# Strassen's algorithm for the second product of an MLP, chunks 1 to 5, in a gated-attention kernel

## The chip, the cores and the metric

The kernel runs on one core of a Trainium2 chip. The metric is the device time of one execution in microseconds. Five engines work side by side, each with a queue of its own that it runs in order: TensorE (PE; its weight loads are listed apart as PEld), VectorE (DVE), ScalarE (ACT), GpSimd (POOL) and SyncE (SP), which here issues the DMAs. They wait for each other through semaphores, which a compiler sets from the program's reads and writes.

## What is computed

A gated linear attention over 768 steps (4 batches, 8 heads of 48), then a layer norm and an MLP with a residual, all in float32; the weights arrive as float64 words and are rounded on the chip.

```python
for t in range(S):
    state = alpha[:, :, t, :, None] * state + np.einsum('bhd,bhe->bhde', k[:, :, t], v[:, :, t])
    y[:, :, t] = np.einsum('bhd,bhde->bhe', q[:, :, t], state)
...
x = np.ascontiguousarray(attn_out.transpose(0, 2, 1, 3)).reshape(B, S, H * D)
xn = (x - mu) / np.sqrt(var + 1e-06) * g_ln
ch = np.maximum(xn @ w_ch1, 0.0) @ w_ch2
return (x + ch).astype(np.float32)
```

Here `x` is 4 x 768 x 384, `w_ch1` is 384 x 1536 and `w_ch2` is 1536 x 384. The change concerns the product by `w_ch2`.

## The kernel before

The 768 steps are cut into six chunks (NCB = 6) of 128 tokens, which is one tile of 128 partitions. For a chunk `c` and a batch `b`, attention goes through five steps:

- `decays` (L184): logarithms of the gates, a prefix sum as a matmul with a triangle of ones (L190), two exponentials on ACT, and the scaled q on DVE (L196) and k on POOL (L195). It also issues the loads of the next chunk.
- `turn` (L206): eight transposes on PE (L211) into two PSUM tiles, copied out into `qkT`.
- `scores` (L219): 48-row matmuls (L226) and two masked copies on DVE (L229).
- `attend` (L233): the output (L240, L245), the new state (L252, L255, L257), `x`, and its layer norm `xn` (L263 to L269).
- `turn_x` (L273): three transposes of `xn` into `xT`.

The MLP of a chunk has twelve `hidden` steps (L284): step `j` multiplies 128 columns of `w1` with the tokens of all four batches, three matmuls of 512 columns (L289), and writes the relu into row `j` of `hT` (ACT at L292, DVE at L294). `hT` is one tile of 128 partitions by [12 j, 4 batches, 128 tokens] with one buffer. `project` (L298) then computes, for one batch, the 128 x 384 output: twelve matmuls (L302), each with a 128 x 128 block of `hT` as the stationary operand and 384 columns of `w2[:, j]` as the moving one, summed in one PSUM tile. It is done in thirds of four matmuls, two batches taking turns. After the last third DVE adds `x` (L306), and SP sends the row out (L307). PSUM has three buffers with the tag `m` for the outputs of `hidden` and `project`, and three with the tag `a` for attention.

The order is written by hand. `run(main, side)` (L325) issues the list `main` and strews the list `side` evenly into it, at most one side step behind each main step here. For chunk `c`, `main` is the projection of `c` and then the hidden steps of `c + 1` (12 + 12 steps), and `side` is the attention of chunk `c + 2` (20 steps), as long as there is one: chunks 0 to 3 have side steps, 4 and 5 have none. Ahead of that loop (L344) stand the attention of chunk 0, the rounding of the weights (`round_weights`, L122, on DVE, six pieces of `w1` and six of `w2`) together with the hidden steps of chunk 0, and the attention of chunk 1 as side steps. The compiler keeps this order as a priority; an engine's instructions may be put ahead of others that would still wait.

Of the kernel before, what the change touches and what calls it, by code (L numbers as in the profile page):

```python
# [9 lines left out]
FP32 = mybir.dt.float32  # L10
INT32 = mybir.dt.int32
UINT32 = mybir.dt.uint32
INT64 = mybir.dt.int64
# [8 lines left out]
def kernel(  # L22
# [8 lines left out]
    w_ch2: bass.AP,  # L31
    out: bass.AP,
):

# [17 lines left out]
    nc = tc.nc  # L54

    B, S, H, D = q.shape
    DM = H * D
    DF = w_ch1.shape[1]
    P = 128
    NCB = S // P  # L60
    NP = H // 2
    R = 64 + D
    NF = DM // P
    NJ = DF // P
# [5 lines left out]
    stage = ctx.enter_context(tc.tile_pool(name="stage", bufs=STAGED))  # L70
    work = ctx.enter_context(tc.tile_pool(name="work", bufs=2))
    dram = ctx.enter_context(
        tc.tile_pool(name="dram", bufs=B, space=bass.MemoryType.DRAM))
    ps = ctx.enter_context(tc.tile_pool(name="ps", bufs=2, space=bass.MemoryType.PSUM))
# [24 lines left out]
    w2 = cpool.tile([P, NJ, DM], FP32, name="w2")  # L99
# [7 lines left out]
    for i in range(NJ // 2):  # L107
        cs, js = slice(2 * i * P, 2 * (i + 1) * P), slice(2 * i, 2 * (i + 1))
# [71 lines left out]
    gate_of, qkT_of, at_of, x_of, xn_of, xT_of, hT_of = ({} for _ in range(7))  # L180
# [23 lines left out]
            load(c + 1, b)  # L204

    def turn(c, b):  # L206
        qkT = work.tile([R, 2, NP, P], FP32, name="qkT", tag="qkT", bufs=3)
        for i in range(2):
            tps = ps.tile([R, NP, P], FP32, name="tps", tag="a", bufs=3)
            for p in range(NP):  # L210
                nc.tensor.transpose(  # L211
                    tps[:, p], qks[b][:, i, p].rearrange("p a b -> p (a b)")[:, :R], ident)
            if i == 0 or c == 1:
                nc.scalar.copy(out=qkT[:, i], in_=tps)  # L214
            else:
                nc.vector.tensor_copy(out=qkT[:, i], in_=tps)
        qkT_of[c, b] = qkT
# [15 lines left out]
    def attend(c, b):  # L233
        qkT, at, vt = qkT_of.pop((c, b)), at_of.pop((c, b)), raws.pop(("v", c, b))
        yps = ps.tile([P, NP, 2, D], FP32, name="yps", tag="s")
        sides = [slice(64 * s, 64 * s + 64) for s in range(2)]
        for p in range(NP):
            if c > 0:
                for s in sides:
                    nc.tensor.matmul(yps[s, p].rearrange("p a b -> p (a b)"), qkT[:, 0, p, s],  # L240
                                     sts[b][:R, p].rearrange("p a b -> p (a b)"),
                                     start=True, stop=False)
            for i in range(2):
                for s in sides:
                    nc.tensor.matmul(yps[s, p, i], at[:, i, p, s], vt[:, 2 * p + i],  # L245
                                     start=(c == 0), stop=(c == 0 or i == 1))
        if c + 1 < NCB:
            sps = ps.tile([R, NP, D], FP32, name="sps", tag="s")
            heads = list(enumerate((slice(0, 64), slice(64, R))))
            for p in range(NP):  # L250
                for i, s in heads:
                    nc.tensor.matmul(sps[s, p], qks[b][:, 1, p, i, :s.stop - s.start],  # L252
                                     vt[:, 2 * p + i], start=True, stop=True)
            for i, s in heads:
                nc.vector.tensor_add(sts[b][s, :, i], sps[s], sts[b][s, :, i])  # L255
            st = sts[b].rearrange("p a b d -> p a (b d)")
            nc.gpsimd.tensor_mul(  # L257
                st, st, gate_of.pop((c, b)).unsqueeze(2).broadcast_to([P, NP, 2 * D]))
        x = work.tile([P, DM], FP32, name="x", tag="x", bufs=3 * B)
        nc.scalar.copy(out=x, in_=yps.rearrange("p a b d -> p (a b d)"))  # L260
        stats = work.tile([P, 6], FP32, name="stats", tag="stats")
        mv = work.tile([P, 2], FP32, name="mv", tag="mv")
        nc.vector.bn_stats(stats, x)  # L263
        nc.vector.bn_aggr(mv, stats)
        rstd = work.tile([P, 1], FP32, name="rstd", tag="rstd")
        nc.scalar.activation(out=rstd, in_=mv[:, 1:2], func=AFT.Ln, bias=eps)
        nc.scalar.activation(out=rstd, in_=rstd, func=AFT.Exp, scale=-0.5)
        xn = work.tile([P, DM], FP32, name="xn", tag="xn", bufs=2)
        nc.vector.tensor_scalar(out=xn, in0=x, scalar1=mv[:, 0:1], scalar2=rstd,  # L269
                                op0=AOP.subtract, op1=AOP.mult)  # L270
        x_of[c, b], xn_of[c, b] = x, xn
# [12 lines left out]
    def hidden(c, j):  # L284
        if j == 0:
            hT_of[c] = work.tile([P, NJ, B, P], FP32, name="hT", tag="hT", bufs=1)
        hps = ps.tile([P, B, P], FP32, name="hps", tag="m", bufs=3)
        for f in range(NF):
            nc.tensor.matmul(hps, w1[:, f, j * P:(j + 1) * P], xT_of[c][:, f],  # L289
                             start=(f == 0), stop=(f == NF - 1))  # L290
        if c == 0 or j % 2 == 0:
            nc.scalar.activation(out=hT_of[c][:, j], in_=hps, func=AFT.Relu)  # L292
        else:
            nc.vector.tensor_scalar_max(hT_of[c][:, j], in0=hps, scalar1=0.0)  # L294
# [3 lines left out]
    def project(c, b, js):  # L298
        if js[0] == 0:
            ops_of[b] = ps.tile([P, DM], FP32, name="ops", tag="m", bufs=3)  # L300
        for j in js:
            nc.tensor.matmul(ops_of[b], hT_of[c][:, j, b], w2[:, j],  # L302
                             start=(j == 0), stop=(j == NJ - 1))
        if js[-1] == NJ - 1:
            ob = work.tile([P, DM], FP32, name="ob", tag="ob", bufs=3)
            nc.vector.tensor_add(ob, ops_of.pop(b), x_of.pop((c, b)))  # L306
            nc.sync.dma_start(out[b, c * P:(c + 1) * P], ob)  # L307

    def attention_steps(c):

        stages = [decays, turn, scores, attend, turn_x]
        return [lambda f=stages[w - b], b=b: f(c, b)
                for w in range(B + len(stages) - 1)
                for b in range(B) if 0 <= w - b < len(stages)]

    def hidden_steps(c):
        return [lambda j=j: hidden(c, j) for j in range(NJ)] if c < NCB else []

    def project_steps(c):

        thirds = [range(i * NJ // 3, (i + 1) * NJ // 3) for i in range(3)]
        return [lambda b=b, js=js: project(c, b, js)
                for b0 in range(0, B, 2) for js in thirds for b in range(b0, min(b0 + 2, B))]

    def run(main, side):  # L325

        done = 0
        for i, step in enumerate(main):
            step()
            due = (i + 1) * len(side) // len(main)  # L330
            for go in side[done:due]:
                go()
            done = due
# [3 lines left out]
    for step in attention_steps(0):  # L337
        step()
    first = hidden_steps(0)
    run([go for i in range(half) for go in (rounds[i], *first[2 * i:2 * i + 2])],  # L340
        attention_steps(1))
    for go in rounds[half:]:
        go()
    for c in range(NCB):  # L344
        side = attention_steps(c + 2) if c + 2 < NCB else []
        run(project_steps(c) + hidden_steps(c + 1), side)


# [27 lines left out]
```

## Time and profile before

| | |
|---|---|
| median of 3 runs | 533.37 us (532.99 to 534.46) |
| the profiled execution's own time | 534.97 us |
| its span (first to last instruction) | 533.3 us |
| granted TensorE clock, mean | 0.99 |
| largest idle time of PE ahead of one group (transposes, L211) | 8.8 us |
| DMA traffic | 33.71 MB, mean 63 GB/s |
| DMA engines' mean busy share in the first slice | 8 tenths |

The profile is of one execution. Its groups give busy time and the mean duration of one instruction; for PE a duration runs from the start of a record to a modelled end, and records of a stream overlap, so that the spacing of a stream comes from the timeline: its length less one duration, divided by its records less one. The sums in the prediction are made against this execution's span of 533.3 us, which lies 1.7 us below its time and happens to equal the median of the runs.

### The profile page before, as it was taken

The page shows a single profiled execution, that of the slowest core. Times are in us where ns is not written, and L with a number is a line of the kernel's source. Part 1 is how long each engine was busy: PE and PEld are TensorE (multiplying, and loading weights), DVE is VectorE, ACT ScalarE, POOL GpSimd, SP SyncE. Part 2 cuts the span into 40 slices and gives each one's busy share as a digit, 9 for nine tenths or more (in the row PEclk, how much of TensorE's full clock was granted, in tenths as well). Part 3 has the DMA queues.
Part 4 walks back from the last instruction along what each step waited for, and adds up shares of the span by engine and source line. Part 5 has one row for each costly group of instructions (what it writes and reads, how often), then busy time and mean ns, then how long its engine had stood idle before and what let it go on. Part 6 is the DMA issues. An engine that isn't in the chain of part 4 may idle for free.

```text
span 533.3 us, 7434 instructions
## 1 busy us (share of the span) xinstructions
PE 510.2 (96%) x3112; PEld 297.9 (56%) x3112; DVE 209.0 (39%) x363; ACT 106.8 (20%) x239; POOL 52.4 (10%) x55
## 2 busy tenths in 40 slices
PE   4877998999999999999999999999999999999997
PEld 2653555556555566654656655556655555544554
DVE  2999899962432313322323324323233220011100
ACT  3452342221212221121121122112112110001000
POOL 3431150010100010010010100001000000000000
PEclk9997998999999999999999999999999999999999
DMA  8976545232110012220013110000000000000000
GB/s 267 300 201 192 172 124 194 76 91 73 59 47 15 17 46 74 76 75 0 16 33 103 31 59 1 1 1 15 16 30 1 1 0 16 15 30 1 0 30 30
DMA packets 32488, 33.71 MB, mean 63 GB/s; under 512 B 13108, under 2 KB 28596, under 8 KB 32456
## 3 DMA queue, kind: packets, MB, share of 16 engines
q1 hardware_dynamic: 31912, 33.12, 20.4%
q8 instruction: 24, 0.39, 0.3%
q10 hardware_dynamic: 544, 0.13, 0.1%
q14 instruction: 8, 0.07, 0.0%
HBM read 28.49 MB, written 4.76 MB: 62 GB/s over the span
## 4 chain that ended last, share of the span: by engine, by line
PE 83%; DVE 11%; DMA 2%; issue 2%; SPq 1%; ACT 0%; DVEq 0%; ACTq 0%
PE ops L302 34%; PE hps L289 33%; PE aps L226 3%; PE tps L211 3%; PE yps L240 3%; PE yps L245 3%; PE lps L190 2%; PE xps L279 1%; DMA ws<-in_moe_w_ch_dram 1%; PE sps L252 1%; DVE w L134 1%; DVE at L229 1%; DVE w L132 1%; DVE st L255 1%; DVE w L146 1%
## 5 line engine op out<-in xcount | busy, mean ns | idle before, releaser
L289 PE MATMUL hps<-xT,w 128*128 128x512 f32 x432 | 199.8, 607 | 0.0
L302 PE MATMUL ops<-w,hT 128*128 128x384 f32 x576 | 194.2, 488 | 0.0
L302 PEld LDWEIGHTS ops<-w,hT 128*128 128x128 f32 x576 | 107.0, 190 | 69.8 <-issue 0.5
L289 PEld LDWEIGHTS hps<-xT,w 128*128 128x128 f32 x432 | 79.6, 193 | 83.3 <-issue 79.0
L196 DVE TENSOR_TENSOR qk<-rq,eq 128x384 f32<-128x384 f32 x24 | 23.8, 990 | 71.1 <-ACT eq L194 71.1
L292 ACT ACTIVATE hT<-hps 128x512 f32<-128x512 f32 x42 | 25.1, 597 | 128.3 <-PE hps L289 128.3
L294 DVE TENSOR_SCALAR hT<-hps 128x512 f32<-128x512 f32 x30 | 20.8, 692 | 73.0 <-PE hps L289 72.6
L195 POOL TENSOR_TENSOR qk<-rk,ek 128x384 f32<-128x384 f32 x24 | 31.2, 1298 | 183.0 <-ACT ek L193 183.0
L306 DVE TENSOR_TENSOR ob<-ops,x 128x384 f32<-128x384 f32 x24 | 13.4, 558 | 78.8 <-PE ops L302 78.8
L229 DVE COPY_PREDICATED at<-consts,aps 128x512 f32<-128x512 int32 x48 | 32.4, 722 | 13.9 <-PE aps L226 13.6
L245 PE MATMUL yps<-rv,at 128*64 128x48 f32 x768 | 36.6, 219 | 0.0
L211 PE MATMUL tps<-consts,qk 128*112 128x128 f32 x192 | 27.4, 284 | 8.8 <-DVE at L229 4.8
L257 POOL TENSOR_TENSOR st<-st,gate 128x384 f32<-128x384 f32 x20 | 17.6, 881 | 160.4 <-DVE st L255 158.2
L211 PEld LDWEIGHTS tps<-consts,qk 128*112 128x112 f32 x192 | 22.4, 138 | 19.5 <-issue 11.4
L245 PEld LDWEIGHTS yps<-rv,at 128*64 128x64 f32 x768 | 32.3, 138 | 1.2 <-issue 1.1
L226 PEld LDWEIGHTS aps<-qkT 48*128 48x128 f32 x384 | 24.4, 193 | 14.0 <-issue 10.6
L255 DVE TENSOR_TENSOR st<-sps,st 64x192 f32<-64x192 f32 (+1 forms) x40 | 14.1, 353 | 41.2 <-PE sps L252 40.9
L240 PE MATMUL yps<-st,qkT 112*64 112x96 f32 x320 | 29.5, 259 | 0.0
L226 PE MATMUL aps<-qkT 48*128 48x128 f32 x384 | 29.3, 291 | 0.1
L214 ACT COPY qkT<-tps 112x512 f32<-112x512 f32 x28 | 16.1, 584 | 56.0 <-PE tps L211 56.0
L193 ACT ACTIVATE ek<-lps 128x384 f32<-128x384 f32 x24 | 11.8, 490 | 69.7 <-PE lps L190 69.5
L190 PE MATMUL lps<-la,consts 128*128 128x384 f32 x48 | 21.1, 524 | 4.4 <-ACT la L188 4.4
(35 smaller groups left out, 250.8 us busy)
## 6 DMA issues: line engine op xcount, KB each, us to landing
ws<-in_moe_w_ch_dram SPq DMA_DIRECT2D x12, 768.0 KB, 5.7
ra<-in_alpha_dram SPq DMA_DIRECT2D x24, 192.0 KB, 3.8
rk<-in_k_dram SPq DMA_DIRECT2D x24, 192.0 KB, 2.4
rq<-in_q_dram SPq DMA_DIRECT2D x24, 192.0 KB, 2.5
rv<-in_v_dram SPq DMA_DIRECT2D x24, 192.0 KB, 3.0
out_dram<-ob SPq DMA_DIRECT2D x24, 192.0 KB, 1.9
row<-eq SPq DMA_DIRECT2D x20, 2.0 KB
gate<-row SPq DMA_DIRECT2D x20, 2.0 KB, 2.9
```

Of the source, the lines that this page charges most:

```text
L190: nc.tensor.matmul(lps[:, :DM], tri, la, start=True, stop=True)
L195: nc.gpsimd.tensor_mul(qk[:, 1, :, :D], raws.pop(("k", c, b)), ek)
L196: nc.vector.tensor_mul(qk[:, 0, :, :D], raws.pop(("q", c, b)), eq)
L211: nc.tensor.transpose(tps[:, p], qks[b][:, i, p].rearrange("p a b -> p (a b)")[:, :R], ident)
L226: nc.tensor.matmul(aps[i][:, p], qkT[rows, 1, p], qkT[rows, 0, p], start=True, stop=True)
L229: nc.vector.copy_predicated(out=at[:, i], data=aps[i], mask=mask.unsqueeze(1).broadcast_to([P, NP, P]))
L240: nc.tensor.matmul(yps[s, p].rearrange("p a b -> p (a b)"), qkT[:, 0, p, s], sts[b][:R, p].rearrange("p a b -> p (a b)"), start=True, stop ...
L245: nc.tensor.matmul(yps[s, p, i], at[:, i, p, s], vt[:, 2 * p + i], start=(c == 0), stop=(c == 0 or i == 1))
L289: nc.tensor.matmul(hps, w1[:, f, j * P:(j + 1) * P], xT_of[c][:, f], start=(f == 0), stop=(f == NF - 1))
L292: nc.scalar.activation(out=hT_of[c][:, j], in_=hps, func=AFT.Relu)
L294: nc.vector.tensor_scalar_max(hT_of[c][:, j], in0=hps, scalar1=0.0)
L302: nc.tensor.matmul(ops_of[b], hT_of[c][:, j, b], w2[:, j], start=(j == 0), stop=(j == NJ - 1))
```

## The change

For chunks 1 to 5 the product by `w2` is done for two batches at a time. Seen as a 2 x 2 block product, the rows are the two batches, the inner axis (1536) falls into two halves of six blocks, and the 384 columns into two halves of 192. Strassen's algorithm (in Winograd's form, with fifteen sums) takes seven products of half size in the place of eight. A product is six matmuls of 192 columns.

- `combine_weights` runs once after chunk 0: four DVE subtractions of 128 x 1152 elements. Three results go into buffers of the weights' staging pool, one over a quarter of `w2`.
- `combine_hidden` runs per pair of batches: four DVE sums of 128 x 768 elements, one of them in place in `hT`, three in a tile with one buffer.
- `product` issues the six matmuls of one product and takes its PSUM tile out: one copy on ACT and six DVE steps with seven adds of 192 columns altogether, and four more adds on POOL. The order is 1, 4, 2, 6, 7, 5, 3. The two output rows go out after products 5 and 3.
- The main list of such a chunk has 14 product steps in the place of 12 thirds. Chunk 0 keeps the old form as `direct_steps`.
- `x` has 9 buffers for 12 and `qkT` 2 for 3.

```diff
-        qkT = work.tile([R, 2, NP, P], FP32, name="qkT", tag="qkT", bufs=3)
+        qkT = work.tile([R, 2, NP, P], FP32, name="qkT", tag="qkT", bufs=2)
...
-        x = work.tile([P, DM], FP32, name="x", tag="x", bufs=3 * B)
+        x = work.tile([P, DM], FP32, name="x", tag="x", bufs=9)
...
+    HJ, HM = NJ // 2, DM // 2
+    win = {}
+
+    def combine_weights():
+        b11, b12 = w2[:, :HJ, :HM], w2[:, :HJ, HM:]
+        b21, b22 = w2[:, HJ:, :HM], w2[:, HJ:, HM:]
+        t1, t2, t4 = (stage.tile([P, NF, 2 * P], INT64, name="ws", tag="ws")
+                      .rearrange("p a c -> p (a c)").bitcast(FP32)[:, :HJ * HM]
+                      .rearrange("p (a c) -> p a c", c=HM) for _ in range(3))
+        nc.vector.tensor_sub(t1, b12, b11)
+        nc.vector.tensor_sub(t2, b22, t1)
+        nc.vector.tensor_sub(t4, b21, t2)
+        nc.vector.tensor_sub(b12, b22, b12)
+        win["b"] = {1: b11, 2: b21, 3: b22, 4: t4, 5: t1, 6: t2, 7: b12}
+
+    def combine_hidden(c, b):
+        hT = hT_of[c]
+        a11, a12, a21, a22 = (hT[:, js, i] for i in (b, b + 1)
+                              for js in (slice(0, HJ), slice(HJ, NJ)))
+        sums = work.tile([P, 3, HJ, P], FP32, name="sums", tag="sums", bufs=1)
+        s2, s3, s4 = (sums[:, i] for i in range(3))
+        nc.vector.tensor_sub(s3, a11, a21)
+        nc.vector.tensor_add(a21, a21, a22)
+        nc.vector.tensor_sub(s2, a21, a11)
+        nc.vector.tensor_sub(s4, a12, s2)
+        win["a"] = {1: a11, 2: a12, 3: s4, 4: a22, 5: a21, 6: s2, 7: s3}
+
+    def product(c, b, n):
+        if n == 1:
+            combine_hidden(c, b)
+            for i in (0, 1):
+                win["o", i] = work.tile([P, 2, HM], FP32, name="ob", tag="ob", bufs=3)
+            for i in range(4):
+                win["u", i] = work.tile([P, HM], FP32, name=f"u{i}", tag=f"u{i}", bufs=1)
+        acc = ps.tile([P, HM], FP32, name="ops", tag="m", bufs=3)
+        for j in range(HJ):
+            nc.tensor.matmul(acc, win["a"][n][:, j], win["b"][n][:, j],
+                             start=(j == 0), stop=(j == HJ - 1))
+        x0, x1 = (x_of[c, i].rearrange("p (s m) -> p s m", s=2) for i in (b, b + 1))
+        o0, o1 = win["o", 0], win["o", 1]
+        p1, u2, u3, u4 = (win["u", i] for i in range(4))
+        add, add_late = nc.vector.tensor_add, nc.gpsimd.tensor_add
+        if n == 1:
+            nc.scalar.copy(out=p1, in_=acc)
+            add_late(o0[:, 0], p1, x0[:, 0])
+        elif n == 4:
+            add(o1[:, 0], acc, x1[:, 0])
+        elif n == 2:
+            add(o0[:, 0], acc, o0[:, 0])
+        elif n == 6:
+            add(u2, acc, p1)
+        elif n == 7:
+            add(u3, acc, u2)
+            add_late(o1[:, 1], u3, x1[:, 1])
+            add_late(o1[:, 0], u3, o1[:, 0])
+        elif n == 5:
+            add(u4, acc, u2)
+            add(o1[:, 1], acc, o1[:, 1])
+            add_late(u4, u4, x0[:, 1])
+            send(c, b + 1, o1)
+        else:
+            add(o0[:, 1], acc, u4)
+            send(c, b, o0)
+            del x_of[c, b], x_of[c, b + 1]
+
+    def send(c, b, ob):
+        nc.sync.dma_start(out[b, c * P:(c + 1) * P], ob.rearrange("p s m -> p (s m)"))
...
     def project_steps(c):
+        if c > 0:
+            return [lambda b=b, n=n: product(c, b, n)
+                    for b in range(0, B, 2) for n in (1, 4, 2, 6, 7, 5, 3)]
+        return direct_steps(c)
+
+    def direct_steps(c):
...
         run(project_steps(c) + hidden_steps(c + 1), side)
+        if c == 0:
+            combine_weights()
```

## The prediction

> **What bounds the kernel now.** I read the page from the top: busy time, slices, chain.
>
> ```profile
> span 533.3 us, 7434 instructions
> PE 510.2 (96%) x3112; PEld 297.9 (56%) x3112; DVE 209.0 (39%) x363; ACT 106.8 (20%) x239; POOL 52.4 (10%) x55
> ...
> PE   4877998999999999999999999999999999999997
> ...
> DVE  2999899962432313322323324323233220011100
> ...
> PE 83%; DVE 11%; DMA 2%; issue 2%; SPq 1%; ACT 0%; DVEq 0%; ACTq 0%
> PE ops L302 34%; PE hps L289 33%; PE aps L226 3%; PE tps L211 3%; PE yps L240 3%; PE yps L245 3%; PE lps L190 2%; PE xps L279 1%; DMA ws<-in_moe_w_ch_dram 1%; PE sps L252 1%; DVE w L134 1%; DVE at L229 1%; DVE w L132 1%; DVE st L255 1%; DVE w L146 1%
> ```
>
> A digit is the busy share of 13.3 us in tenths. TensorE (PE) is full from the eighth slice (93 us) on; VectorE (DVE) is full before that, and from the tenth slice (120 us) on mostly at two to four tenths. The chain of what ended last is 83% PE, and 34% of the span is the line that changes, L302. But a busy PE need not be a PE at its peak, so I ask next how its records follow each other. The window of a middle chunk, three timelines' rows, and the groups by shape:
>
> ```profile
> 186.10:270.00 83.90, 83.89 (x540) 49.22 (x537) 26.23 (x46) 16.78 (x38) 7.31 (x8) 1.00 0.17 48
> ```
> ```profile
> 436.64 0.69 DVE L294 TENSOR_SCALAR hT<-hps 128x512 f32<-128x512 f32 x1 [0.40 <-PE hps L289]
> 436.66 30.62 PEld L302 LDWEIGHTS ops<-w,hT 128*128 128x128 f32 x96
> 436.76 31.13 PE L302 MATMUL ops<-w,hT 128*128 128x384 f32 x96
> ```
> ```profile
> 474.60 24.20 PE L289 MATMUL hps<-xT,w 128*128 128x512 f32 x56
> ```
> ```profile
> L289 PE MATMUL hps<-xT,w 128*128 128x512 f32 x432 | 199.8, 607 | 0.0
> L302 PE MATMUL ops<-w,hT 128*128 128x384 f32 x576 | 194.2, 488 | 0.0
> L302 PEld LDWEIGHTS ops<-w,hT 128*128 128x128 f32 x576 | 107.0, 190 | 69.8 <-issue 0.5
> ```
>
> The columns of a window are its length, then busy time of PE, PEld, DVE, ACT and POOL with counts, the clock, and the DMAs. PE works 83.89 of 83.90 us, at the full clock (1.00), DVE 26.23. There are 576 records for 288 float32 matmuls (6 chunks x 4 batches x 12 blocks of K), so a matmul is two records. One record lasts 488 ns but overlaps the next: 96 of them (one chunk) take 31.13 us, and (31.13 - 0.49) / 95 = 0.3226 us from start to start. With 512 columns it is (24.20 - 0.61) / 55 = 0.4289 us. The difference of 128 columns is 0.1063 us, 0.831 ns a column, which leaves 322.6 - 384 x 0.831 = 3.4 ns fixed. So the kernel streams columns with hardly a gap, and fewer columns are time saved, if the short matmuls still hide their weight loads.
>
> **The matmuls.** A pair of batches has today 2 x 12 matmuls of 384 columns: 48 records x 0.3226 = 15.48 us. After it: 7 products x 6 matmuls of 192 columns, 84 records. With the line above one record takes 192 x 0.831 + 3.4 = 163 ns, a product (12 records) 1.96 us, a pair 84 x 0.163 = 13.69 us. That is 1.79 us a pair, and 5 chunks x 2 pairs give **17.9 us**. PE's records of L302 go from 576 to 96 + 840.
>
> No 192-column stream stands in the trace, so what its loads do has to be bounded. The near rows:
>
> ```profile
> 127.55 2.74 PE L302 MATMUL ops<-w,hT 128*128 128x384 f32 x8
> ...
> 132.42 2.85 PE L302 MATMUL ops<-w,hT 128*128 128x384 f32 x8
> ...
> 138.97 1.04 PE L211 MATMUL tps<-consts,qk 128*112 128x128 f32 x8
> 138.98 0.79 PEld L211 LDWEIGHTS tps<-consts,qk 128*112 128x112 f32 x7 [0.19 <-issue]
> ```
> ```profile
> L211 PE MATMUL tps<-consts,qk 128*112 128x128 f32 x192 | 27.4, 284 | 8.8 <-DVE at L229 4.8 <-DVE qk L196 3.9 <-PE aps L226 0.2
> ```
>
> The same eight records take 2.74 us in the middle of a stream and 2.85 right behind an attention step: one load stands exposed there, for 0.11 us. And eight transposes, each with a load of its own, take 1.04 us: (1.04 - 0.28) / 7 = 0.109 us a record, which is 128 x 0.831 + 3.4 = 0.110, with no surcharge for the load. A load of 0.11 us fits below 0.163. The ends: 0.161 (half of 0.3226) and 0.190 (the load's duration, if loads did not overlap each other). I take 0.163, by the transposes.
>
> [...]
>
> **The sums on DVE.** Prices of DVE and GpSimd (POOL):
>
> ```profile
> 109.67 0.55 DVE L196 TENSOR_TENSOR qk<-rq,eq 128x384 f32<-128x384 f32 x1
> ...
> 111.12 0.96 DVE L142 SCALAR_TENSOR_TENSOR w<-w,ws 128x768 f32<-128x768 f32 x1
> ```
> ```profile
> L257 POOL TENSOR_TENSOR st<-st,gate 128x384 f32<-128x384 f32 x20 | 17.6, 881 | 160.4 <-DVE st L255 158.2 <-DMA rk<-in_k_dram 2.1
> ...
> L306 DVE TENSOR_TENSOR ob<-ops,x 128x384 f32<-128x384 f32 x24 | 13.4, 558 | 78.8 <-PE ops L302 78.8
> ...
> L132 DVE TENSOR_SCALAR w<-ws 128x768 int32<-128x768 int32 x12 | 8.8, 744 | 0.3 <-DMA ws<-in_moe_w_ch_dram 0.3
> ...
> L255 DVE TENSOR_TENSOR st<-sps,st 64x192 f32<-64x192 f32 x20 | 6.9, 346 | 40.9 <-PE sps L252 40.9
> ```
>
> Two inputs of 384 cost 0.55 us, of 768 0.96. The four sums of combine_hidden (768 elements) are 3.8 us a pair. The evictions become one ScalarE copy and seven DVE adds of 192 from PSUM (0.35 each by L255, 2.4 us) for two of 0.56, plus four POOL adds of about 0.45 (half of L257). DVE gains about 5.1 us a pair, 10.3 a chunk, on 26.23 of 83.90: it stays far from full. What matters is when.
>
> Time 0 is the start of product 1, which needs no sum. Products 4 and 2 need none of combine_hidden either, so product 6 is the first to wait for one (s2, the third), at 3 x 1.96 = 5.87 us. At a chunk's start the last relu ends 0.57 us after time 0 (436.64 + 0.69 against 436.76), and three sums later it is 3.45. In the second pair the sums have one buffer, free when product 3 has ended: 0.2 for its end, 0.35 for its add, 2.9 for three sums, again 3.45. Two microseconds are spare, and a POOL add beside a sum takes at most half a microsecond of that (an L196 beside POOL takes 1.08 for 0.55, a row below). The fourth sum and product 4's eviction end near 4.8; that PSUM buffer is wanted by product 7 at 7.8. Cost 0; if the cover goes, every microsecond beyond it costs ten.
>
> That product 1 doesn't wait for the sum written in place beside its operand (a21, rows between those of a11) needs dependencies by region. The L132 row shows them: it writes columns of w1 interleaved with those PE is reading, and in 12 times it waited 0.3 us, for a DMA.
>
> **The weight sums**, once, are four of 1152 elements: 0.55 + 2 x 0.41 = 1.37 us each. Held to their place in the code, the third would end 0.57 + 4.1 = 4.7 us after time 0 of chunk 1, where product 4 wants it at 1.96: 2.7 us. But the chain of the start shows DVE taking work ahead of the code's order:
>
> ```profile
> 16.51 0.95 DVE w L132
> ...
> 34.22 0.47 DVE xn L269
> ```
>
> The rounding stands behind the whole first attention in the code, and runs before its end. So the weight sums should fall into DVE's idle time in chunk 0, from 120 us on by the slices. I take 0.7, between 0 and 2.7.
>
> **Attention between products.** The steps are the same; but a product covers less than a third of a projection did (8 records, 2.58 us).
>
> ```profile
> 191.97 2.74 PE L302 MATMUL ops<-w,hT 128*128 128x384 f32 x8
> ...
> 193.13 1.08 DVE L196 TENSOR_TENSOR qk<-rq,eq 128x384 f32<-128x384 f32 x1 [6.64 <-ACT eq L194]
> ...
> 194.55 1.04 PE L211 MATMUL tps<-consts,qk 128*112 128x128 f32 x8
> ```
>
> The first turn of a chunk follows the first decays by one step. L196 ends at 194.21, the transposes start as soon as the stream ends, 194.55. With 1.96 us of cover PE would be free at 193.93 and wait about 0.45 us: chunks 1 to 3, 1.3 us. For other collisions in these six pairs I put 0.7 (between 0 and 9, the partial rival). The fewer buffers (x, qkT) cost nothing: the buffer each needs was read by work already ahead of it on PE, or by the pair before. SyncE gets as many output DMAs as now, one of them a product earlier. The tail has an add of 0.35 for 0.56: 0.2 saved.
>
> **Sum.** -17.9 - 0.2 + 0.7 + 1.3 + 0.7 = -15.4. The profiled execution took 534.97 us with a span of 533.3; 15.4 off that is 519.6. It lay 1.6 above the median of 533.37, against which the same sum gives **518.0 us**.
>
> **Rivals.**
> Partial loss: each pair has one sum's worth of wait (0.95 us), because DVE is held by attention (it waits there in order for ScalarE's and PE's results) when the sums should start. 518.0 + 9 = 527. For it: DVE runs its work in order, and L196 above stood 6.64 us until ScalarE had written eq; against: two microseconds of slack, and chunks 4 and 5 have no attention.
>
> Late sums, slower: product 1 or 6 waits at every pair for relu and two or more sums, 0.57 + 1.9 and more, about 2.8 us; ten pairs give 28, so 533.4 - 18.1 + 28 = 543. It decides from 1.8 us a pair. Against it speaks the L132 row.
>
> Loads set the spacing: a record takes the load's 0.190 us. 840 x 0.190 = 159.6 against 480 x 0.3226 = 154.8: 4.8 us more, and with the losses 2.5, 540.7, slower; equal from 0.184 on. For it: L302's loads last 190 ns. Against it: the 0.109 us of the transposes. [...]
>
> The gain is eaten evenly by small waits, so that nothing is seen (1.8 us a pair): 533.
>
> **Chances.** Forecast (514.5 to 521) 0.71; partial loss (521 to 529) 0.12; late sums 0.08; loads 0.05; nothing seen 0.04. A measurement of this kernel tells about 0.3% (1.6 us) from no change. Faster 0.83, same 0.04, slower 0.13. The range, 514.5 to 527, takes in no loss at all with 0.161 us a record (513.9, cut a little) and most of the partial loss, some 0.8 in all.
>
> **What would show it.** Right: a chunk's project stage without attention (chunk 5) takes 168 records at 0.163, 27.4 us for 31.1, with no idle PE; the sums' line waits on PE, not PE on it; the weight sums run before chunk 1. Wrong: records 0.18 us apart; PE idle released by DVE at the product's line, at the first or fourth product of a pair; transposes released by L196 for more than 0.5 us; a first stage (to 100 us) that is longer than now.

## The result and the profile after

| | before | after |
|---|---|---|
| median of the runs | 533.91 us (532.99 to 534.64, 4 runs) | 517.18 us (515.80 to 518.33, 4 runs) |
| ratio to before, 95% interval | | 0.9686 (0.9654 to 0.9719) |
| span of the profiled execution | 533.3 us | 513.8 us |

The change takes 16.7 us off the median. From the page of the changed kernel: the span, the busy times, the slices of PE, PEld and DVE, and the chain.

```profile
span 513.8 us, 8361 instructions
PE 490.8 (96%) x3472; PEld 343.3 (67%) x3472; DVE 265.4 (52%) x457; ACT 109.6 (21%) x249; POOL 84.6 (16%) x95
...
PE   4887998999999999999999999999999999999997
PEld 2764555556655579965579975569985559954697
DVE  2999999993523365633354733335643224412342
...
PE hps L292 34%; PE ops L350 26%; PE ops L305 5%; PE aps L229 4%; PE tps L214 4%; PE yps L243 3%; PE yps L248 3%; PE lps L193 2%; DVE qk L199 2%; PE xps L282 1%; DVE at L232 1%; PE sps L255 1%; DVE st L258 1%; DVE w L149 1%; DVE w L135 1%
```

PE is as full as before and has 360 records more, but is busy 19 us less, about 17.5 of them behind the start of the first projection. DVE has 56 us more work and stays at one to seven tenths after the start. In the slices that the products fill, weight loads are now busy nine tenths of the time. The changed line is L350; the old form stays for chunk 0 (L305).

Where the time went is seen by stages: the windows of the projections of chunks 1, 2, 3, 4 and 5, each from its first matmul to the first of the next hidden step. The columns are the window's length, busy time of PE, PEld, DVE, ACT and POOL with counts, PE's clock, and the DMAs. Before, with chunk 0's projection ahead of them:

```profile
100.16:143.08 42.92, 42.01 (x230) 26.28 (x229) 22.77 (x37) 7.70 (x19) 4.99 (x5) 1.00 0.23 65
186.16:227.30 41.14, 41.14 (x226) 26.05 (x225) 12.36 (x20) 7.06 (x16) 3.83 (x4) 1.00 0.22 63
...
436.76:467.73 30.97, 30.97 (x99) 18.25 (x97) 2.24 (x4) 0.48 (x1) 0.00 (x0) 1.00 0.05 20
```
```profile
270.39:311.53 41.14, 41.14 (x227) 26.06 (x225) 12.36 (x20) 7.06 (x16) 3.83 (x4) 1.00 0.19 54
354.62:395.30 40.68, 40.68 (x211) 25.59 (x210) 11.65 (x18) 6.65 (x15) 3.00 (x3) 1.00 0.04 15
498.63:529.75 31.12, 31.12 (x97) 18.05 (x95) 2.37 (x4) 0.00 (x0) 0.00 (x0) 1.00 0.05 19
```

After, likewise:

```profile
97.28:141.16 43.88, 42.21 (x230) 26.24 (x228) 27.91 (x41) 7.70 (x19) 8.04 (x5) 1.00 0.23 64
184.24:222.12 37.88, 37.70 (x299) 35.31 (x297) 22.19 (x37) 8.99 (x21) 11.13 (x13) 1.00 0.24 69
...
424.81:452.11 27.30, 27.30 (x170) 27.30 (x169) 12.23 (x21) 1.12 (x3) 5.39 (x8) 1.00 0.05 18
```
```profile
483.01:510.48 27.47, 27.47 (x169) 27.16 (x167) 12.13 (x21) 0.64 (x2) 5.61 (x8) 1.00 0.05 20
265.14:302.96 37.82, 37.69 (x298) 35.30 (x297) 22.29 (x37) 8.99 (x21) 11.20 (x13) 1.00 0.20 58
345.98:383.34 37.36, 37.23 (x283) 34.84 (x281) 21.50 (x35) 8.16 (x19) 10.38 (x12) 1.00 0.05 17
```

The five projections lose 3.26, 3.32, 3.32, 3.67 and 3.65 us, 17.2 together. Chunks 4 and 5, which have no attention, have no idle PE at all: 30.97 became 27.30. Chunk 0's projection, which the change leaves in its old form, takes 43.88 for 42.92 us, 1.0 more. With 0.2 saved behind the last matmul and 0.2 in the hidden steps that makes 16.6 from the first projection to the end of the span (433.1 and 416.5 us); the medians differ by 16.7. The spans differ by more, 19.5 us, because this one execution reached its first projection at 97.28 us and the one of before at 100.16. Over the ten kernels profiled in this study that moment lies between 97.3 and 101.3 us, and the six others that have the changed kernel's code up to there reach it between 98.6 and 101.3: the start differs from execution to execution, while the stages of chunks 1 to 5 repeat to a hundredth or two where their code is the same.

### The profile page after: what moved, and what is told of

It reads as the page before. It is cut to its first block, busy times and chain, and to the rows that moved or that the text cites. A ratio compares the mean times of both kernels' runs of the same rounds, so it can differ in the third digit from the quotient of the medians.

```text
span 513.8 us, 8361 instructions
## 1 busy us (share of the span) xinstructions
PE 490.8 (96%) x3472; PEld 343.3 (67%) x3472; DVE 265.4 (52%) x457; ACT 109.6 (21%) x249; POOL 84.6 (16%) x95
## 4 chain that ended last, share of the span: by engine, by line
PE 82%; DVE 11%; issue 3%; DMA 1%; POOL 1%; ACT 1%; SPq 0%; POOLq 0%; DVEq 0%; ACTq 0%
PE hps L292 34%; PE ops L350 26%; PE ops L305 5%; PE aps L229 4%; PE tps L214 4%; PE yps L243 3%; PE yps L248 3%; PE lps L193 2%; DVE qk L199 2%; PE xps L282 1%; DVE at L232 1%; PE sps L255 1%; DVE st L258 1%; DVE w L149 1%; DVE w L135 1%
## 5 line engine op out<-in xcount | busy, mean ns | idle before, releaser
L198 POOL TENSOR_TENSOR qk<-rk,ek 128x384 f32<-128x384 f32 x24 | 36.1, 1505 | 89.0 <-ACT ek L196 89.0
L350 PE MATMUL ops<-w,sums 128*128 128x192 f32 x240 | 42.9, 329 | 0.0
L350 PE MATMUL ops<-w,hT 128*128 128x192 f32 x240 | 42.3, 326 | 0.0
L350 PE MATMUL ops<-ws,hT 128*128 128x192 f32 x240 | 42.3, 326 | 0.0
L350 PEld LDWEIGHTS ops<-w,sums 128*128 128x128 f32 x240 | 39.4, 190 | 2.3
L350 PEld LDWEIGHTS ops<-w,hT 128*128 128x128 f32 x240 | 39.3, 190 | 1.3 <-issue 0.5
L350 PEld LDWEIGHTS ops<-ws,hT 128*128 128x128 f32 x240 | 39.5, 190 | 0.8
L305 PE MATMUL ops<-w,hT 128*128 128x384 f32 x96 | 33.2, 490 | 0.0
L258 DVE TENSOR_TENSOR st<-sps,st 64x192 f32<-64x192 f32 (+1 forms) x40 | 14.1, 354 | 36.3 <-PE sps L255 36.0
```

The costliest lines, as they stand in the source:

```text
L198: nc.gpsimd.tensor_mul(qk[:, 1, :, :D], raws.pop(("k", c, b)), ek)
L305: nc.tensor.matmul(ops_of[b], hT_of[c][:, j, b], w2[:, j], start=(j == 0), stop=(j == NJ - 1))
L350: nc.tensor.matmul(acc, win["a"][n][:, j], win["b"][n][:, j], start=(j == 0), stop=(j == HJ - 1))
```

## The experiments

**The buffers alone.** Is the earlier start due to the change's two smaller buffer counts?

```diff
-        qkT = work.tile([R, 2, NP, P], FP32, name="qkT", tag="qkT", bufs=3)
+        qkT = work.tile([R, 2, NP, P], FP32, name="qkT", tag="qkT", bufs=2)
...
-        x = work.tile([P, DM], FP32, name="x", tag="x", bufs=3 * B)
+        x = work.tile([P, DM], FP32, name="x", tag="x", bufs=9)
```

> The kernel before with nothing but the change's buffer counts (x 9 for 12, qkT 2 for 3). In the changed kernel's profile the first projection starts at 97.28 us and in the profile of before at 100.16, so 2.9 of the 19.5 us between the two spans lie ahead of the changed code. Theory: buffers cost and bring nothing, and the 2.9 us are the spread of single executions or of the start's order: ratio 1.000 +- 0.003 against before. Rival: two qkT buffers put the start in a better order: 2 to 3 us faster (0.995), and the first projection starts near 97 us.

Measured: 534.29 us, ratio to before 0.9998 (0.9977 to 1.0019); the first projection starts at 100.12 us. The windows up to it and of chunk 0's projection:

```profile
0.00:100.12 100.12, 81.72 (x750) 51.45 (x750) 87.00 (x156) 35.86 (x80) 24.21 (x26) 0.97 0.66 201
100.12:143.01 42.89, 42.00 (x229) 26.27 (x228) 22.75 (x37) 7.70 (x19) 4.99 (x5) 1.00 0.23 65
```

The buffers do nothing. The 1.0 us that chunk 0 lost is not theirs either: with them alone its projection takes 42.89.

**Halves of 192 columns without Strassen.** Do the half-size matmuls themselves gain or cost?

```diff
+    def project_half(c, b, m, js):
...
+        cols = slice(m * DM // 2, (m + 1) * DM // 2)
+        for j in js:
+            nc.tensor.matmul(ops_of[b][:, cols], hT_of[c][:, j, b], w2[:, j, cols],
+                             start=(j == 0), stop=(j == NJ - 1))
...
```

> The kernel before with the product of chunks 1 to 5 cut into two halves of 192 columns, each a group of 12 matmuls with its own weight loads, but without Strassen: 8 products' worth, 96 records a pair. Theory (a record of 192 columns streams in 0.1625 us and hides its load): 96 x 0.1625 = 15.60 us a pair against 15.48, so 1.2 us slower over ten pairs, 534 to 536. Rival (the shorter matmuls cost something that the seven products hide, or they themselves bring the gain): 5 us or more away from before, either way.

Measured: 538.23 us, ratio to before 1.0085 (1.0053 to 1.0117). Chunk 4's projection:

```profile
439.65:470.86 31.21, 31.21 (x195) 31.21 (x194) 2.24 (x4) 0.48 (x1) 0.00 (x0) 1.00 0.05 17
```

192 records in 31.21 us are 0.1625 us each, 0.24 us a chunk over the old form (30.97). That is the price of halving, and Strassen's 27.30 is 0.875 of 31.21: seven eighths to the third digit. The time rose more than expected all the same. By stages 2.4 us can be placed: 0.5 in chunks 4 and 5, and 0.65 in each of chunks 1 to 3, where the projection gives 1.0 and the hidden steps take 0.3 back, since the side steps fall otherwise and a turn waits 0.19 us. Of the rest, 0.3 lies behind the last matmul (3.84 us for 3.51), and the first projection's start at 101.10 us accounts for 0.9 in this execution; what is left of the 4.2 us between the medians is not placed.

**Twice the loads.** How near is the load's floor?

```diff
-        for j in range(HJ):
-            nc.tensor.matmul(acc, win["a"][n][:, j], win["b"][n][:, j],
-                             start=(j == 0), stop=(j == HJ - 1))
+        for m in (slice(0, HM // 2), slice(HM // 2, HM)):
+            for j in range(HJ):
+                nc.tensor.matmul(acc[:, m], win["a"][n][:, j], win["b"][n][:, j, m],
+                                 start=(j == 0), stop=(j == HJ - 1))
```

> The changed kernel with each product's 192 columns done as two groups of 96, so twice the weight loads for the same columns: 168 records a pair. If only columns set the time, a record takes 96 x 0.831 + 3.4 = 0.083 us, a pair 13.98, and the time rises by 3 us to about 520. If a load of about 0.105 us is the floor of a record, a pair takes 168 x 0.107 = 18.0 us against 13.65, and the time rises by 43 us to about 560. If loads did not overlap each other (0.190 us each), a pair takes 31.9 us and the time is near 700. Theory: the second.

Measured: 567.95 us in one run. Products of chunk 4 in the timeline, and the group:

```profile
461.79 2.84 PE L351 MATMUL ops<-w,hT 128*128 128x96 f32 x24
464.47 2.84 PE L351 MATMUL ops<-ws,sums 128*128 128x96 f32 x24
```
```profile
L351 PE MATMUL ops<-w,sums 128*128 128x96 f32 x480 | 57.1, 276 | 0.0
```

A product of 24 records takes 464.47 - 461.79 = 2.68 us, 0.1117 a record, and not the 0.083 that 96 columns need by the prediction's line. So a record of this stream with its 128x128 load has a floor of 0.112 us, about two thirds of what 192 columns give it, and PE reaches it without a gap (37.49 us busy in chunk 4's 37.49). It is no floor of every record: eight records of 48 columns with loads of 64 (L245 of the kernel before) take 0.39 us together, (0.39 - 0.22) / 7 = 0.02 apart. That it is the load's is argued from this, and not tested alone. The second theory holds (50.8 us more than the changed kernel's median, expected 43; the floor is 0.112 and not 0.107). A second level of Strassen, with 96 columns, would by these rows lie on this floor.

**Without the sums.**

```diff
-        sums = work.tile([P, 3, HJ, P], FP32, name="sums", tag="sums", bufs=1)
-        s2, s3, s4 = (sums[:, i] for i in range(3))
-        nc.vector.tensor_sub(s3, a11, a21)
-        nc.vector.tensor_add(a21, a21, a22)
-        nc.vector.tensor_sub(s2, a21, a11)
-        nc.vector.tensor_sub(s4, a12, s2)
-        win["a"] = {1: a11, 2: a12, 3: s4, 4: a22, 5: a21, 6: s2, 7: s3}
+        win["a"] = {1: a11, 2: a12, 3: a12, 4: a22, 5: a21, 6: a21, 7: a11}
```

> The changed kernel without the four sums of combine_hidden; products 3, 5, 6 and 7 take blocks of hT in their place, so the output is not the reference's. 3.9 to 4.3 us of DVE work a pair go. Theory: all of it lies beside PE, the time falls by 0 to 1 us (0.998 to 1.000 of the changed kernel, 516 to 518). Rival (the sums or their waits still eat part of the gain): 3 us or more faster than the changed kernel, below 514.

Measured: 518.33 us, ratio to before 0.9706 (0.9677 to 0.9734); no faster than with the sums. Chunks 1 and 4:

```profile
188.23:226.12 37.89, 37.70 (x299) 35.31 (x298) 15.29 (x30) 8.98 (x21) 9.47 (x13) 1.00 0.24 69
428.82:456.12 27.30, 27.30 (x170) 27.30 (x169) 5.04 (x14) 1.11 (x3) 4.63 (x8) 1.00 0.05 18
```

DVE has 7 us less in each window, and the windows are as long as with the sums (37.88 and 27.30). From the first projection to the end it is 416.5 us with them and without. Their cost is nothing that these stages show; the median lies 0.3 us above the range that was expected.

**Later sums.** From where would they cost? Three, and in another run six, sums more stand ahead of s2; they are written into s2 and overwritten.

```diff
+        for _ in range(3):
+            nc.vector.tensor_sub(s2, a12, a22)
         nc.vector.tensor_sub(s2, a21, a11)
```

> The changed kernel with three sums more ahead of s2 (128 x 768, written into s2 and then overwritten), 2.9 us more of DVE ahead of product 6 in each pair. In the changed kernel's chunk 4 s2 is ready at 427.36 us and product 6 starts at 430.66, 3.3 us later; in the second pair the room is about 4.3. Theory (the sums cost nothing until they come later than product 6): chunk 4's projection stays at 27.3 us, chunks 1 to 3 gain under 1 us each by attention work held up on DVE, the time is that of the changed kernel plus 0 to 3. Rival (each microsecond of DVE work costs a part of itself): 29 us of it in all show as 5 us or more, evenly over the chunks.

Measured: 521.96 us in one run; chunk 4's projection takes 28.48, not 27.3. Its timeline around product 6 of each pair (the rows with ws,sums), and DVE's ahead of the second of them:

```profile
432.35 2.11 PE L352 MATMUL ops<-w,hT 128*128 128x192 f32 x12
434.41 2.19 PE L352 MATMUL ops<-ws,sums 128*128 128x192 f32 x12
...
446.18 2.11 PE L352 MATMUL ops<-w,hT 128*128 128x192 f32 x12
449.05 2.19 PE L352 MATMUL ops<-ws,sums 128*128 128x192 f32 x12 [0.75 <-DVE sums L338]
```
```profile
447.69 0.35 DVE L362 TENSOR_TENSOR ob<-ops,x 128x192 f32<-128x192 f32 x1
447.96 0.95 DVE L338 TENSOR_TENSOR sums<-hT 128x768 f32<-128x768 f32 x1
```

Products follow each other at 1.95 us, so product 6 is 0.11 late in the first pair and 0.92 in the second, and each wait leaves one load exposed (2.19 for 2.11). The expectation had the second pair's room wrong: I had counted it from product 4 instead of product 1. Counted rightly it is 2.4 us in the changed kernel (s2 ready at 441.95, product 6 at 444.31), so 2.9 us more must make it late by half a microsecond. Product 4's eviction (L362), which stood behind s2 before, now stands ahead of it and adds 0.3. These parts of the miss are mine; that a wait appears where the room ends is what the theory says.

The whole took 4.8 us more than the changed kernel's median, where 0 to 3 were expected, and 5.1 by the stages. Chunks 1 to 3 make 2.1 of it: the turn behind their first decays waits 0.8 to 0.9 us for DVE's scaled q, where it waited 0.13 to 0.18. Chunks 4 and 5 make 2.8, at product 6, and chunk 0, which has none of these sums, 0.3. So the total is of the size that the rival gave, but it isn't spread evenly as the rival has it; it stands where PE waits for DVE.

> As the run before with six sums more, 5.75 us in each pair, beyond the room. Theory: product 6 waits 2.4 us in a chunk's first pair and 1.4 in the second, chunk 4's projection takes 27.3 + 3.9 = 31.2 us and is as long as before the change (30.97), and the whole is 18 to 30 us slower than the changed kernel, so 535 to 547, no faster than before. Rival: twice the excess of the run before.

Measured: 552.65 us in one run, over 5 us beyond the range. PE's waits, chunk 4's first product 6 in the timeline, and its windows:

```profile
PE ops L352 <- DVE sums L338: 18.7, 7, 3.9
```
```profile
446.69 3.87 PE L352 MATMUL ops<-ws,sums 128*128 128x192 f32 x12 [3.06 <-DVE sums L338]
```
```profile
437.61:446.90 9.29, 6.23 (x39) 5.96 (x38) 9.08 (x12) 0.80 (x2) 1.32 (x1) 1.00 0.00 0
446.90:450.20 3.30, 3.30 (x11) 3.30 (x11) 0.64 (x1) 0.00 (x0) 0.00 (x0) 0.50 0.00 0
450.20:467.40 17.20, 13.33 (x82) 13.06 (x82) 11.66 (x17) 0.32 (x1) 2.82 (x4) 1.00 0.06 24
467.40:470.70 3.30, 3.30 (x12) 3.30 (x11) 0.36 (x1) 0.00 (x0) 0.00 (x0) 0.50 0.00 0
```

The waits stand at product 6 of a pair, as expected (18.7 us in 7 that the profile names, up to 3.9). What was not expected is in the clock's column: behind each of the two long waits PE runs at half its clock for some 3.3 us, and the first of these products 6 takes 3.87 us for 2.11. Chunk 4's projection grew by 10.8 us, to 38.08; the idle time ahead of product 6 in its two pairs makes 6.9 of it (3.06 and 3.87), half the clock about 3.4 of the rest. The rival's twice the excess of three sums would be some 10 us; it is 35. So DVE's work was free up to a point here (27.30 us in chunk 4 with the four sums and without) and dear behind it (28.48 with three more, 38.08 with six).

**The weight sums later.** Why did chunk 0's projection take 1.0 us more? In the changed kernel's timeline of that stage:

```profile
104.91 1.34 DVE L322 TENSOR_TENSOR ws<-w 128x1152 f32<-128x1152 f32 x1
...
105.11 4.27 POOL L198 TENSOR_TENSOR qk<-rk,ek 128x384 f32<-128x384 f32 x1 [5.41 <-ACT ek L196]
...
109.44 0.65 PE L214 MATMUL tps<-consts,qk 128*112 128x128 f32 x4 [1.08 <-POOL qk L198]
```

POOL's product of k takes 4.27 us there and 1.00 to 1.02 in 15 of its 24 places, and the turn waits for it. In the kernel before it takes 1.33 at this place, though DVE has hardly a gap there either; what is new is the first weight sum, which starts 0.2 us ahead of it. The experiment makes the sums wait for chunk 0's projection:

```diff
-        nc.vector.tensor_sub(t1, b12, b11)
-        nc.vector.tensor_sub(t2, b22, t1)
-        nc.vector.tensor_sub(t4, b21, t2)
         nc.vector.tensor_sub(b12, b22, b12)
+        nc.vector.tensor_add(t2, b12, b11)
+        nc.vector.tensor_sub(t1, b22, t2)
+        nc.vector.tensor_sub(t4, b21, t2)
```

> The changed kernel with the four weight sums in another order that gives the same blocks: first the one over a quarter of w2, which must wait for the last read of chunk 0's projection, then the three that need its result. They can then not be taken while DVE is still full with rounding. In the changed kernel the first runs at 104.91 us, GpSimd's k product comes late behind it, the second half of a turn waits 1.08 us at 109.44, and chunk 0's projection takes 43.88 us against 42.92 before. Theory: it takes 42.9 again, 1.0 us less, and chunk 1 stays at 37.9; ratio to the changed kernel 0.998. Rival (the longer first projection comes from the buffers or another order): 43.9 stays.

Measured: 518.27 us, ratio to before 0.9706 (0.9689 to 0.9723). Projections of chunks 0 and 1, and POOL's product of k:

```profile
100.31:143.22 42.91, 42.01 (x230) 26.28 (x228) 27.72 (x41) 7.71 (x19) 4.99 (x5) 1.00 0.23 65
186.31:224.19 37.88, 37.69 (x299) 35.30 (x297) 22.18 (x37) 8.99 (x21) 11.13 (x13) 1.00 0.25 69
```
```profile
108.15 1.33 POOL L198 TENSOR_TENSOR qk<-rk,ek 128x384 f32<-128x384 f32 x1 [5.42 <-ACT ek L196]
```

Chunk 0 takes 42.91 again, as before the change, and the sums, now at 134 to 141 us, delay nothing in chunk 1. The earlier start of the changed kernel's execution is not the cause: the run below, with chunk 0's second pair, reaches its first projection at 101.33 us, later than the kernel before (100.16), and the product beside its early sum takes 6.00. The runs with twice the loads and with three and six sums more, which leave the weight sums as the changed kernel has them, show its one wait for POOL's product too, 1.1 us in each. Without a weight sum there the stage takes 42.92 us (the kernel before), 42.89 (the buffers alone) and 42.91 (this run), and the product 1.33 in the first and the last of them. By the stage this form is 1.0 us better than the changed kernel. The timed runs can't tell them apart, since the start varies by more (100.31 us in this execution).

**Chunk 0's second pair too.** Could half of chunk 0 gain as well?

```diff
+        seven = [lambda b=b, n=n: product(c, b, n)
+                 for b in range(0, B, 2) for n in (1, 4, 2, 6, 7, 5, 3)]
...
-        return direct_steps(c)
+        return direct_steps(c)[:6] + [combine_weights] + seven[7:]
...
-        if c == 0:
-            combine_weights()
```

> The changed kernel with Strassen's seven products for the second pair of chunk 0 too, the weight sums placed behind its first pair. Theory: the weights are rounded and their sums taken (113.6 us in the changed kernel) before the second pair begins near 119, so it saves 1.8 us of chunk 0's 43.88, and what is left is 42.1 to 42.6; ratio to the changed kernel 0.997. Rival: the quarter of w2 that is overwritten, or DVE, comes late, and product 6 or 7 waits: 44 or more.

Measured: 521.27 us, ratio to before 0.976 (0.9735 to 0.9784), slower than the changed kernel. Chunk 0's projection takes 45.32 us. Its timeline has the same wait again, longer:

```profile
109.16 6.00 POOL L198 TENSOR_TENSOR qk<-rk,ek 128x384 f32<-128x384 f32 x1 [5.41 <-ACT ek L196]
```
```profile
115.22 1.10 PE L214 MATMUL tps<-consts,qk 128*112 128x128 f32 x4 [2.80 <-POOL qk L198]
```

The rival had the outcome right and the place wrong. No product waits; DVE gets a sum of hT (L334, at 112.50 us) into its full stretch as well, POOL's product of k takes 6.0 us, and PE stands 2.8 us. That the sum of hT is what lengthens it from 4.27 to 6.00 is likely by its place, but no run tests it alone. In the window from 114.8 to 118.1 us the granted clock is 0.50. The pair's 1.8 us are lost to the wait and the slow stretch. The stage explains 1.4 of the 4.1 us by which the median lies above the changed kernel's; the rest isn't placed (this execution reached its first projection at 101.33 us).

## Why the prediction held, by its steps

**The matmuls: right.** 0.163 us a record were forecast, 0.1625 is measured: a product starts 1.95 us after the one ahead of it (424.81, 426.76, 428.71). The stages without attention lose 3.66 us a chunk, 1.83 a pair against 1.79. The rival by which loads set the spacing falls: 0.1625 and not 0.19. What was measured lies on the line through 384 and 512 columns (192 x 0.831 + 3.4 = 163 ns), with nothing added for the load. Only the records of 96 columns took longer than that line gives, 0.1117 us for 0.083.

**The sums on DVE: right.** The changed kernel's chunk 4 from DVE's and from PE's side:

```profile
424.69 0.69 DVE L297 TENSOR_SCALAR hT<-hps 128x512 f32<-128x512 f32 x1 [0.34 <-PE hps L292]
425.41 0.96 DVE L335 TENSOR_TENSOR hT<-hT 128x768 f32<-128x768 f32 x1
426.40 0.96 DVE L336 TENSOR_TENSOR sums<-hT 128x768 f32<-128x768 f32 x1
427.39 1.37 DVE L337 TENSOR_TENSOR sums<-hT,sums 128x768 f32<-128x768 f32 x1
```
```profile
424.81 2.12 PE L350 MATMUL ops<-w,hT 128*128 128x192 f32 x12
426.76 2.11 PE L350 MATMUL ops<-ws,hT 128*128 128x192 f32 x12
428.71 2.11 PE L350 MATMUL ops<-w,hT 128*128 128x192 f32 x12
```

s2 (L336) is ready at 427.36, 2.55 us behind product 1's start where 3.45 was forecast: the sum that needs only the first half of hT (s3, L334) had gone ahead into the hidden steps. In the second pair, where it can't, s2 is ready 3.49 us behind product 1 (441.95 against 438.46), as forecast. Product 1 starts at 424.81, ahead of the sum written in place beside its operand (L335, 425.41), so the dependencies go by region here. Without the sums the stages are as long; with six sums more PE waits. Late sums and partial loss both fall.

**The weight sums: the place wrong, the size near by luck.** 0.7 us were taken, 1.0 is measured. They don't fall into the idle time from 120 us on: the first is taken at 104.91, while DVE is full, and PE pays in chunk 0, behind POOL. The prediction had looked only at DVE and product 4 for the price; that another cause cost about as much was luck.

**Attention between products: right, too dear.** The turn behind the first decays waits 0.18, 0.13 and 0.13 us in chunks 1 to 3 where 0.45 each was put. Those chunks gain 3.26, 3.32 and 3.32 us against 3.66 without attention, so all collisions cost 1.1 us, for 2.0 in the sum.

**The tail: right.** The end of the span lies 3.31 us behind the last matmul's end, 3.51 before.

So the sum forecast -15.4, and the stages give -17.2 + 1.0 - 0.2 - 0.2 = -16.6, the last term from the hidden steps, for which the sum had nothing; the medians give -16.7. Most of the difference is the 0.9 that the collisions fell short of their term.

## What to carry to other kernels

In these streams without gaps fewer columns were time saved (0.3226 us a record with 384, 0.1625 with 192) down to a floor (0.112 with 96, for 0.083); elsewhere the point is found by halving once more. The sums that the change put on DVE were free up to their first consumer (product 6, 0.92 us late with three sums more), or that of the work queued behind them there (the turn, 0.8 to 0.9 us in the same run), so put the products that need no sum ahead of those that do, and count the room from the start of the first. When one engine is full, look also at the engine beside it: here the price of a sum on DVE was paid by GpSimd's instruction (4.27 us for 1.33), and through it by PE (a wait of 1.08 us).

## What the runs showed of the hardware

PE's clock halved behind some waits. In the run with six sums more, waits of 3.06 and 3.87 us in chunk 4 were each followed by a stretch at 0.50; the twelve records of the row above take 3.71 us to the next product's start (446.69 to 450.40), 0.31 each and not 0.1625. A wait's length alone doesn't decide it. 2.80 us in chunk 0 was followed by such a stretch (the run with chunk 0's second pair, 0.50 from 114.8 to 118.1 us), and so was 1.66 us once in the run with six sums more (0.50 from 385.5 to 388.7). In the run with three sums more, waits of 2.9 us for xn and 3.3 us for the masked copy were not: its mean clock is 1.000. Here is the stretch around that second wait (1.54 and 1.79 us idle, 3.33 together) in three windows, and then, in two, the same place in the kernel before, where PE waited 3.09 us (79.05 to 82.14):

```profile
76.40:79.81 3.41, 1.87 (x14) 0.92 (x12) 3.38 (x8) 1.46 (x4) 0.83 (x1) 1.00 0.71 231
79.81:83.23 3.42, 1.63 (x7) 1.06 (x8) 3.39 (x6) 0.59 (x1) 0.00 (x0) 1.00 0.43 66
83.23:86.64 3.41, 3.41 (x11) 1.42 (x9) 3.41 (x7) 0.97 (x2) 0.00 (x0) 1.00 0.44 171
```
```profile
79.52:82.94 3.42, 0.80 (x5) 0.68 (x6) 3.39 (x6) 0.82 (x3) 0.00 (x0) 1.00 0.87 284
82.94:86.35 3.41, 3.41 (x8) 1.59 (x7) 3.41 (x7) 0.88 (x2) 0.00 (x0) 0.50 0.56 216
```

The clock's entries in the traces of the two kernels, which begin 14.7 us (before) and 14.1 us (after) into the span, show a grid behind this. In the kernel before, the slow stretches start at 41.98 and 82.94 us, 12 x 3.413 us apart, and last 6.83 and 3.41 us; in the changed kernel they start at 41.41 and 78.96, 11 x 3.413 apart, and last 3.41 each. One more entry of half the clock, behind the last instruction, lies 132 x 3.413 us from the second stretch before (533.50) and 128 x 3.413 after (515.87). The first slow stretch of each starts ahead of the end of PE's wait (2.89 us, to 42.67, before; 2.88, to 41.49, after), so it is not the wait's end that sets it off. In the cells of 3.41 us ahead of the slow stretches PE's rows, with their modelled ends, leave 2.25 and 2.61 us idle before (38.56:41.98 and 79.52:82.94) and 2.81 and 2.48 after (38.00:41.41 and 75.55:78.96). The other full-speed cells of the two profiles, from the clock's first entry to PE's last work, leave 1.37 us or less, and the next cell is at 1.00; behind a slow cell with 0.70 us idle (41.98:45.39, before) the next was slow again. The cell in which the changed kernel's last matmul ends leaves 1.97 us (509.04:512.46), and the clock is at 1.00 from there to the end of the span. What amount is enough these two profiles don't show. Whether the three windows of the run with three sums more are cells of its grid isn't shown either, as no slow stretch falls within its work; if they are, its 3.33 us fell on two of them, with less idle time in each than in the four cells above.

A GpSimd instruction with two inputs, the product of k, mostly takes 1.0 us, but 4.27 or 6.00 where it starts beside a weight sum on a full DVE (the rows of L198 above). A full DVE alone doesn't decide it: at 108.15 us in the run with the sums late it takes 1.33. Earlier, while DVE rounds weights, the same product takes 6.08 us in the kernel before (at 69.31) and 6.09 in the changed one (at 66.74). Why it is slow there isn't shown; at the early sum's place the rows show no more than that the weight sum stands beside the slow ones.
